# Rows of a mixture of experts moved as quarters of 96 words, turned by VectorE instead of TensorE

## The chip, the cores and the metric

The kernel runs on one core of one Trainium2 chip. The metric is device time of one execution in microseconds (us); the time shown is a median of three runs. The engines are TensorE (PE, with its weight loads PEld), VectorE (DVE), ScalarE (ACT), GpSimd (POOL) and SyncE (SP), which here only issues DMAs.

## The reference

Two stages in float32. The first is a gated recurrence for 4 batches, 8 heads, 768 steps, head size 48. Its output, as 3072 token rows of 384 words, goes through a two-level gate to one of 4 x 4 experts with 1024 hidden units.

```python
# stage 1, for each batch and head
state = alpha[t][:, None] * state + outer(k[t], v[t])
y[t] = q[t] @ state
# x = y as (3072, 384); stage 2
g_idx = argmax(x @ w_group);  g_w = softmax weight of g_idx
for g in range(4):
    e_idx = argmax(xg @ w_expert[g]);  e_w = its softmax weight
    for e in range(4):
        h = maximum(xg[mask_e] @ w1[g, e], 0.0)
        out[tok_idx] = (g_w * e_w)[:, None] * (h @ w2[g, e])
```

## The kernel before

The recurrence runs in 24 chunks of 128 steps, four batches one after the other. For each chunk the kernel forms 128 token rows of `xr` (`[128, 24, XW]`, 384 words, then the token's weight, then its number). The gate's choice gives every token a place in a table `slots_d` in device memory, one stretch of 3072 rows for each expert, and `scatter` writes the 128 rows of a chunk with one indirect DMA issued by POOL. Unused places were filled beforehand from `blank` with a token number out of range, so that such rows are not written in the end.

The experts follow as 17 jobs. Jobs 0 and 1 are both expert 0: its first 128 rows, which are read back early into `early_rows`, and up to 96 more. Jobs 2 to 16 are the other 15 experts in falling order of their counts, with room for 216 tokens in job 2, three fewer from job to job and 168 in the last. A loop after them takes what is left over; on this input it has no turn. For job j the program does this:

- `fetch_rows` (L768, SP) reads the job's rows, tokens on partitions, three jobs ahead; `load_weights` (L169, L171, SP) reads the weights, two jobs ahead, as soon as the buffer of job j - 2 is free.
- `columns` calls `turned` (L617): six TensorE transposes bring up to 2 x 112 rows into a layout with features on partitions; DVE copies them from PSUM to `xt_e` (L619). In the program this stands after `hidden` of the job before.
- `dst` (L804, DVE) is the row numbers for the output as integers, in one of two buffers.
- `hidden` (L632): 96 matmul rows of the profile's kind in four groups, each read by ACT's ReLU (L634) into `hT`. `result` (L647): 96 more, copied by ACT into `yT` (L649).
- `deliver_last` stands behind the first group of the next job's `hidden`: six transposes of `yT` back into rows (L659), two DVE multiplications by the weight (L664), two indirect DMAs from POOL into the output (L666).

Each engine works in program order (the order is written out by hand, no scheduler moves anything). SP's DMAs all go through one queue, POOL's indirect DMAs through another, and both are carried by the same 16 DMA engines.

Of the kernel before, what the change touches and what calls it, by code (L numbers as in the profile page):

```python
# [34 lines left out]
def gla_then_hierarchical_moe(  # L35
# [60 lines left out]
    XW = DM + 2  # L96
# [37 lines left out]
    part_f = iota("part_f", [P, 1], [[0, 1]], cm=1)  # L134
    token_f = iota("token_f", [P, NT], [[P, NT]], cm=1)
# [11 lines left out]
    nc.gpsimd.memset(blank.rearrange("p (t w) -> p t w", t=2)[:, :, DM + 1:XW], float(N))  # L147
# [6 lines left out]
    nc.gpsimd.tensor_copy(out=xr[:, :, DM + 1], in_=token_f)  # L154

    early_rows = cp.tile([P, FIXED, XW], F32, name="early_rows")
# [38 lines left out]
    with ExitStack() as gla:  # L195
# [175 lines left out]
        def to_rows(n, yt):  # L371
# [17 lines left out]
            if n + 1 == LAST:  # L389
                logits()  # L390
            nc.scalar.copy(out=x[:, bc, 0:DM].rearrange("s (p w) -> s p w", p=HP),
                           in_=z[:, :, 0:D2])
# [3 lines left out]
        def choose(b, c0, c1):  # L396
# [46 lines left out]
            nc.vector.reciprocal(out=x[:, c0:c1, DM], in_=cw)  # L443

        def send(b, c0, c1):
# [32 lines left out]
            def scatter(c):  # L478
# [134 lines left out]
    def turned(xg, xt, n, c0, copy=nc.vector.tensor_copy):  # L613

        z = bank()
        for dc in range(DC):
            nc.tensor.transpose(z[:, dc * P:dc * P + n], xg[0:n, dc * P:(dc + 1) * P],  # L617
                                ident[0:n, 0:n])
        copy(  # L619
            out=xt[:, :, c0:c0 + n],  # L620
            in_=z[:, 0:DM].rearrange("p (c t) -> p c t", c=DC)[:, :, 0:n])
# [16 lines left out]
    def result(w2, hT, n):  # L638

        yT = mp.tile([P, DC, CAP], F32, name="yT")  # L640
# [12 lines left out]
    out_by = deque(dram_disjoint_views(out, 2 * NE + 1))  # L653

    def deliver(yT, c0, n, weight, dst, by_act=False):
# [4 lines left out]
        yo = mp.tile([P, DM], F32, name="yo", bufs=3)  # L660
        if by_act:
            nc.scalar.activation(out=yo[0:n], in_=zy[0:n, 0:DM], func=AF.Copy, scale=weight)
        else:
            nc.vector.tensor_scalar(out=yo[0:n], in0=zy[0:n, 0:DM], scalar1=weight,  # L664
                                    scalar2=None, op0=ALU.mult)
# [4 lines left out]
    def columns(job, *copies):  # L670
        xt = mp.tile([P, DC, CAP], F32, name="xt_e")
        for t, (c0, n) in enumerate(job["parts"]):
            turned(job["rows"][:, t, :], xt, n, c0, *copies[t:t + 1])
        return xt

    def left_over():
# [20 lines left out]
        for of, total in ((excess, held), (ceiling, base)):  # L697
# [8 lines left out]
        nc.vector.tensor_scalar(out=first, in0=first, scalar1=float(P), scalar2=part_f,  # L706
                                op0=ALU.mult, op1=ALU.add)
        gone = rp.tile([P, NX], F32, name="gone")
        nc.vector.tensor_tensor(out=gone, in0=first, in1=held, op=ALU.is_ge)
        nc.vector.tensor_tensor(out=first, in0=base, in1=first, op=ALU.add)  # L710
        nc.vector.scalar_tensor_tensor(out=first, in0=gone, scalar=float(NE * N), in1=first,
                                       op0=ALU.mult, op1=ALU.add)
        n_more = rp.tile([P, 1], I32, name="n_more")
        nc.vector.tensor_copy(out=n_more, in_=ends[:, NE - 1:NE])
        return first, whose, n_more
# [35 lines left out]
    jobs = [dict(e=e, parts=[(0, EARLY)], rows=early_rows[:, e:e + 1, :]) for e in range(FIXED)]  # L751
    jobs += [dict(e=e, parts=[(0, CAP - EARLY)]) for e in range(FIXED)]
    jobs += [dict(r=r, parts=[(0, BLK), (BLK, cap(r) - BLK)]) for r in range(NS)]
# [9 lines left out]

    def fetch_rows(job):
        e, k = expert(job), len(job["parts"])
        c0, n = (EARLY, CAP - EARLY) if k == 1 else (0, BLK)
        job["rows"] = mp.tile([P, 2, XW], F32, name="xg", bufs=5)
        return nc.sync.dma_start(  # L768
            out=job["rows"][0:n, 0:k, :],
# [140 lines left out]
```

## Time and profile before

| | |
|---|---|
| three runs | 447.63, 448.93, 449.02 us; median 448.93 |
| profiled execution, its own time | 447.46 us |
| span of the profile, first to last instruction | 445.6 us |
| PE busy | 412.8 us (93% of the span) |
| DVE, ACT, POOL busy | 150.8, 124.9, 149.3 us |
| mean granted TensorE clock | 0.968 of full speed |
| moved by DMA | 95.35 MB, 214 GB/s on average |

The times below and in the rows are from the start of the span. The recurrence takes about the first 150 us, the expert jobs the rest, job 2 starting at 178.44 and job 16 at 418.52. The profiled execution is 1.47 us below the median of the runs, so sums are made against 447.46.

### The profile page before, as it was taken

To read this page: it belongs to the slowest core of one execution; us is meant where nothing else is said; L and a number is where in the kernel's file an instruction comes from. 1 tells how busy PE (TensorE), PEld (TensorE's weight loads), DVE (VectorE), ACT (ScalarE), POOL (GpSimd) and SP (SyncE) were. 2 spreads that over 40 slices of the span, in tenths; PEclk is the share of its full clock that TensorE was granted. 3 is DMA by queue.
4 is the path that set the end of the run, shared out by engine and by line. 5 is a ranking of instruction groups with operands and counts; after the bars stand their busy time and mean duration, and the time that the engine had idled before them with its cause. 6 is when DMAs were issued, how large, how long until landed. Compare 5 with 4: busy or idle time off the path is not lost.

```text
span 445.6 us, 8826 instructions
## 1 busy us (share of the span) xinstructions
PE 412.8 (93%) x3538; PEld 392.5 (88%) x3538; DVE 150.8 (34%) x437; ACT 124.9 (28%) x306; POOL 149.3 (34%) x197
## 2 busy tenths in 40 slices
PE   5998998988989797999999999999999999999990
PEld 4887887877878697999999999999999999999990
DVE  7768667678864620101172101011011011111100
ACT  1464645455556211211112111112112111112110
POOL 6886649579767500001201011022021012021111
PEclk9998988899989899999999999999999999999996
DMA  8999975696112369557546565586576486574000
GB/s 264 403 370 360 350 317 195 212 359 251 38 37 91 107 233 352 199 193 272 192 159 230 220 237 201 172 282 219 170 273 237 168 299 219 193 264 171 6 20 24
DMA packets 22506, 95.35 MB, mean 214 GB/s; under 512 B 5119, under 2 KB 9740, under 8 KB 17984
## 3 DMA queue, kind: packets, MB, share of 16 engines
q1 hardware_dynamic: 16448, 85.27, 53.2%
q0 software_dynamic: 6016, 9.50, 6.3%
q8 instruction: 29, 0.48, 0.5%
q14 instruction: 13, 0.11, 0.1%
HBM read 79.73 MB, written 15.10 MB: 213 GB/s over the span
## 4 chain that ended last, share of the span: by engine, by line
issue 57%; PE 21%; POOL 10%; DVE 7%; ACT 1%; DMA 1%; POOLq 0%; ACTq 0%; DVEq 0%
POOL out_dram L666 7%; PE bank L380 4%; PE bank L349 4%; PE bank L284 4%; PE bank L361 3%; PE bank L321 2%; DVE cq L270 2%; PE bank L309 1%; DVE rev L262 1%; PE bank L632 1%; POOL sm L297 1%; POOL qp L272 1%; POOL kp L265 1%; PE bank L164 1%; DVE gained L329 1%
## 5 line engine op out<-in xcount | busy, mean ns | idle before, releaser
L632 PE MATMUL bank<-xt_e,w 128*128 128x128 f32 (+16 forms) x816 | 136.4, 325 | 1.9 <-ACT xt_e L619 1.9
L632 PEld LDWEIGHTS bank<-xt_e,w 128*128 128x128 f32 x816 | 130.8, 193 | 2.3 <-ACT xt_e L619 2.3
L647 PE MATMUL bank<-hT,w 128*128 128x128 f32 (+16 forms) x816 | 132.5, 322 | 0.0
L647 PEld LDWEIGHTS bank<-hT,w 128*128 128x128 f32 x816 | 128.8, 190 | 0.1
L666 POOL DMA_INDIRECT out_dram<-yo,dst x32 | 36.7, 1148 | 243.3 <-DVE yo L664 228.2
L634 ACT ACTIVATE hT<-bank 128x256 f32<-128x256 f32 (+16 forms) x68 | 32.6, 479 | 112.1 <-PE bank L632 109.2
L664 DVE TENSOR_SCALAR yo<-bank,xg 112x384 f32<-112x384 f32 (+15 forms) x30 | 17.2, 611 | 116.0 <-PE bank L659 116.0
L649 ACT COPY yT<-bank 128x192 f32<-128x192 f32 (+32 forms) x34 | 13.3, 390 | 124.5 <-PE bank L647 124.5
L619 DVE COPY xt_e<-bank 128x336 f32<-128x336 f32 (+15 forms) x30 | 12.4, 456 | 83.0 <-PE bank L617 83.0
L284 PE MATMUL bank<-qp,kp 48*128 48x128 f32 x384 | 32.0, 302 | 5.6 <-POOL qp L272 5.6
L297 POOL TENSOR_SCALAR_AFFINE_SELECT sm<-sm 128x512 f32<-128x512 f32 x43 | 26.3, 632 | 28.1 <-ACT sm L296 28.1
L284 PEld LDWEIGHTS bank<-qp,kp 48*128 48x128 f32 x384 | 25.6, 199 | 10.2 <-POOL qp L272 5.8
L361 PE MATMUL bank<-sm,v 128*48 128x128 f32 (+1 forms) x384 | 31.9, 301 | 0.4
L380 PE MATMUL bank<-wr,yt 112*128 112x116 f32 x192 | 28.1, 291 | 1.3 <-ACT yt L368 1.1
L296 ACT COPY sm<-bank 128x512 f32<-128x512 f32 x43 | 23.3, 588 | 15.4 <-PE bank L284 13.8
L361 PEld LDWEIGHTS bank<-sm,v 128*48 128x48 f32 (+1 forms) x384 | 25.2, 144 | 2.6 <-POOL sm L297 1.2
L480 POOL DMA_INDIRECT slots_d<-xr,place x24 | 24.2, 1008 | 9.1 <-issue 4.5
L380 PEld LDWEIGHTS bank<-wr,yt 112*128 112x128 f32 x192 | 23.9, 196 | 3.7 <-ACT yt L368 2.5
L349 PE MATMUL bank<-qp,state 48*48 48x128 f32 (+1 forms) x320 | 24.6, 299 | 0.0
L270 DVE TENSOR_TENSOR_SCAN cq<-qka,starts 112x387 f32<-112x387 f32 x24 | 23.0, 959 | 2.5
L337 ACT ACTIVATE state<-gained,rev 112x48 f32<-112x48 f32 x64 | 16.2, 323 | 25.9 <-DVE gained L329 21.7
L272 POOL TENSOR_TENSOR qp<-qka,cq 112x384 f32<-112x384 f32 x24 | 21.9, 912 | 2.7 <-DVE cq L270 2.4
(116 smaller groups left out, 320.7 us busy)
## 6 DMA issues: line engine op xcount, KB each, us to landing
w<-in_w_dram SPq DMA_DIRECT2D x32, 1536.0 KB, 7.3
qka<-in_qka_dram SPq DMA_DIRECT2D x24, 578.0 KB, 9.7
slots_d<-blank SPq DMA_DIRECT2D x1, 5404.0 KB, 20.3
xg<-slots_d SPq DMA_DIRECT2D x15, 337.8 KB, 7.8
v<-in_v_dram SPq DMA_DIRECT2D x3, 1152.0 KB, 12.5
w<-in_qka_dram SPq DMA_DIRECT2D x4, 578.0 KB, 9.2
w<-in_qka_dram SPq DMA_DIRECT2D x4, 385.5 KB, 5.7
w<-in_qka_dram SPq DMA_DIRECT2D x4, 193.0 KB, 3.3
```

What stands on the lines that cost most here:

```text
L270: nc.vector.tensor_tensor_scan(out=flat(cq), data0=a[:, 0:W], data1=st, initial=1.0, op0=ALU.mult, op1=ALU.min)
L272: nc.gpsimd.tensor_tensor(out=qp, in0=q, in1=cq[:, :, 1:A1], op=ALU.mult)
L284: nc.tensor.matmul(z[i][:, p * P:(p + 1) * P], lhsT=kp[r, p, c, :], rhs=qp[r, p, c, :], start=True, stop=True)
L297: nc.gpsimd.affine_select(out=sm[:, i], in_=sm[:, i], pattern=[[0, HP], [1, P]], compare_op=ALU.is_ge, fill=0.0, base=0, channel_multiplie ...
L349: nc.tensor.matmul(z[o, p * P:(p + 1) * P], lhsT=st[r, p, 0:o.stop - o.start], rhs=qp[r, p, c, :], start=(p == 0), stop=False, skip_group_ ...
L361: nc.tensor.matmul(z[o, p * P:(p + 1) * P], lhsT=vs[b][:, bc, h * D:h * D + o.stop - o.start], rhs=sm[:, i, p, :], start=(p == 0 and bc == ...
L380: nc.tensor.matmul(z[:, p * W:(p + 1) * W], lhsT=yt[:, p, :], rhs=wr[:, p, :], start=True, stop=True)
L480: nc.gpsimd.indirect_dma_start(out=slots_by[t], out_offset=bass.IndirectOffsetOnAxis(ap=place[:, c:c + 1], axis=0), in_=x[:, c0 + c, :], i ...
L632: nc.tensor.matmul(z[:, k * n:(k + 1) * n], lhsT=w1[:, dc, f * P:(f + 1) * P], rhs=xt[:, dc, 0:n], start=(dc == 0), stop=(dc == DC - 1))
L634: nc.scalar.activation(out=hT[:, f0:f0 + 2, 0:n], in_=z[:, 0:2 * n].rearrange("p (f t) -> p f t", f=2), func=AF.Relu)
L647: nc.tensor.matmul(z[:, i * n:(i + 1) * n], lhsT=w2[:, f, dc * P:(dc + 1) * P], rhs=hT[:, f, 0:n], start=(f == 0), stop=(f == FC - 1))
L666: nc.gpsimd.indirect_dma_start(out=out_by.popleft(), out_offset=bass.IndirectOffsetOnAxis(ap=dst, axis=0), in_=yo[0:n], in_offset=None, bo ...
```

## The change

A token's row in `slots_d` becomes four quarters of 96 words, each followed by its own copy of the weight and its own number (`4 * token + quarter`): 392 words instead of 386. A job's rows are read with one DMA for each quarter, so that partition `32 j + t` holds quarter j of token t of each block of 32 tokens (`[128, blocks, 98]`; seven blocks for jobs 2 to 9, six for jobs 10 to 16). One VectorE instruction then transposes all the squares of 32 x 32 of a job; the feature order that results is other than before, and the host permutes the rows of `w1` and the columns of `w2` to suit. On the way back one VectorE transpose turns `yT` into quarters, one multiplication applies the weights, and each block of 32 tokens is written with an indirect DMA of 128 quarters of 96 words. Only the last job goes back as before, through TensorE, with a small extra load (`marks`) of weights and numbers. `yT` is two fixed buffers, zeroed once by POOL.

```diff
-    XW = DM + 2
+    QW = DM // 4 + 2
+    XW = 4 * QW
+    NB = CAP // 32
...
-    part_f = iota("part_f", [P, 1], [[0, 1]], cm=1)
-    token_f = iota("token_f", [P, NT], [[P, NT]], cm=1)
+    for j in range(4):
+        z = slice(32 * j, 32 * j + 32)
+        nc.gpsimd.iota(out=in_tile[z], pattern=[[32, 4]], base=0, channel_multiplier=1,
+                       allow_small_or_imprecise_dtypes=True)
+        nc.gpsimd.memset(quarter[z], float(j))
+    quarter_f = iota("quarter_f", [P, NT, 4], [[4 * P, NT], [1, 4]], cm=4)
...
-                    for e in range(FIXED):
-                        nc.sync.dma_start(out=early_rows[:, e, :],
-                                          in_=slots_d[e * N:e * N + EARLY, :])
+                    for j in range(4):
+                        nc.sync.dma_start(
+                            out=early_rows[32 * j:32 * j + 32],
+                            in_=slots_d[0:EARLY, j * QW:(j + 1) * QW].rearrange(
+                                "(b t) w -> t b w", t=32))
...
+    results = [rp.tile([P, DC, CAP], F32, name=f"yT{i}") for i in range(2)]
+    for t in results:
+        nc.gpsimd.memset(t, 0.0)
...
+    def deliver_quarters(job, yT, dst):
+
+        nb, rows = job["nb"], job["rows"]
+        yq = mp.tile([P, NB, DM // 4], F32, name="yq")
+        nc.vector.transpose(
+            out=yq[:, 0:nb].rearrange("p b (c r) -> p b c r", c=DC),
+            in_=yT[:, :, 0:32 * nb].rearrange("p c (b t) -> p b c t", t=32))
+        nc.vector.tensor_tensor(
+            out=yq[:, 0:nb], in0=yq[:, 0:nb],
+            in1=rows[:, 0:nb, QW - 2:QW - 1].to_broadcast([P, nb, DM // 4]), op=ALU.mult)
+        for b in range(nb):
+            nc.gpsimd.indirect_dma_start(
+                out=out_by.popleft().rearrange("n (j w) -> (n j) w", j=4),
+                out_offset=bass.IndirectOffsetOnAxis(ap=dst[:, b:b + 1], axis=0),
+                in_=yq[:, b, :], in_offset=None, bounds_check=4 * N - 1, oob_is_err=False)
 
-    def columns(job, *copies):
+    def columns(job):
         xt = mp.tile([P, DC, CAP], F32, name="xt_e")
-        for t, (c0, n) in enumerate(job["parts"]):
-            turned(job["rows"][:, t, :], xt, n, c0, *copies[t:t + 1])
+        nb = job["nb"]
+        nc.vector.transpose(
+            out=xt[:, :, 0:32 * nb].rearrange("p c (b t) -> p b c t", t=32),
+            in_=job["rows"][:, 0:nb, 0:DM // 4].rearrange("p b (c r) -> p b c r", c=DC))
         return xt
+
+    def destined(job):
+
+        nb, left = job["nb"], job["n"] % 32
+        dst = mp.tile([P, NB], I32, name="dst_q")
+        nc.vector.tensor_copy(out=dst[:, 0:nb], in_=job["rows"][:, 0:nb, QW - 1])
+        if left:
+            none = mp.tile([P, 1], F32, name="none")
+            nc.vector.tensor_scalar(out=none, in0=in_tile[:, 0:1], scalar1=float(left),
+                                    scalar2=float(4 * N), op0=ALU.is_ge, op1=ALU.mult)
+            nc.vector.tensor_tensor(out=dst[:, nb - 1:nb], in0=none,
+                                    in1=job["rows"][:, nb - 1, QW - 1:QW], op=ALU.add)
+        return dst
...
     def fetch_rows(job):
...
+        job["rows"] = mp.tile([P, NB, QW], F32, name="xq", bufs=5)
+        of = slots_d.rearrange("(e n) w -> e n w", e=NE)[ds(e, 1)]
+        for j in range(4):
+            dma = nc.sync.dma_start(
+                out=job["rows"][32 * j:32 * j + 32, 0:nb, :],
+                in_=of[:, c0:c0 + 32 * nb, j * QW:(j + 1) * QW].rearrange(
+                    "o (b t) w -> (o t) b w", t=32))
```

On TensorE an expert job before reads as follows (job 3, from its first matmul to the start of `result`; L632 is `hidden`, L659 the way back of job 2, L617 the way in of job 4).

```order
L632 MATMUL bank<-xt_e,w_2338 128x213 [waits DMAHW5_49,DVE_49]
L632 MATMUL bank<-xt_e,w_2338 128x213 x5
L659 MATMUL bank<-ident,yT 112x128 [waits Activation_49]
...
L659 MATMUL bank<-ident,yT 104x128 x2
L632 MATMUL bank<-xt_e,w_2338 128x213 [waits PE_49]
...
L617 MATMUL bank<-ident,xg 128x112 [waits DMAHW4_49,PE_49]
L617 MATMUL bank<-ident,xg 128x112 x2
L617 MATMUL bank<-ident,xg 128x98 [waits Activation_49]
L617 MATMUL bank<-ident,xg 128x98 x2
L647 MATMUL bank<-hT,w_2339 128x213 [waits DMAHW6_49,DVE_49]
```

And with the change, the same job (L639 is `hidden`, L655 `result`).

```order
L639 MATMUL bank<-xt_e,w_2362 128x213 [waits DMAHW4_49,DVE_49,PE_49]
L639 MATMUL bank<-xt_e,w_2362 128x213 x5
L639 MATMUL bank<-xt_e,w_2362 128x213 [waits PE_49]
...
L655 MATMUL bank<-hT,w_2363 128x213 [waits DMAHW5_49,Activation_49]
L655 MATMUL bank<-hT,w_2363 128x213
L655 MATMUL bank<-hT,w_2363 128x213 [waits Activation_49]
```

All twelve transposes are gone, and TensorE no longer waits itself for the rows' DMA.

On VectorE the same stretch reads with the change as follows: the transposes of the rows (L701), the output numbers (L710 to L715), the way back of the job before (L686, L689).

```order
L701 STREAM_TRANSPOSE xt_e<-xq 128x7x3x32 [waits DMAHW2_49,DMAHW1_49,DMAHW3_49,DMAHW0_49,PE_49]
L710 CAST dst_q<-xq 128x7 [waits DMASW4_49,DMASW3_49,DMASW5_49,DMASW2_49,DMASW7_49,DMASW1_49,DMASW0_49]
L713 TENSOR_SCALAR none<-in_tile 128x1
L715 TENSOR_TENSOR dst_q<-none,xq 128x1 [waits DVE_49]
L686 STREAM_TRANSPOSE yq<-yT_2160 128x672 [waits Activation_49]
L689 TENSOR_TENSOR yq<-yq,xq 128x672 [waits DVE_49]
L701 STREAM_TRANSPOSE xt_e<-xq 128x7x3x32 [waits DMAHW6_49,DMAHW1_49,DMAHW7_49,DMAHW0_49,PE_49]
```

The copy into `dst_q` waits for POOL's seven scatters (DMASW) that last used its buffer, those of two jobs before; behind it on VectorE stand the way back of the job before and the columns of the next.

On POOL the end of the first stage before reads as follows: the last two scatters of rows into `slots_d`, then the first one into the output.

```order
L480 DMA slots_d<-xr,place 49152x386 [waits DMASW6_49,Activation_49]
L480 DMA slots_d<-xr,place 49152x386 [waits DMASW7_49,DVE_49,Activation_49]
L666 DMA out_dram<-yo,dst 3072x384 [waits DMASW0_49,DVE_49,Pool_49]
```

With the change the two fixed `yT` buffers are cleared between them.

```order
L490 DMA slots_d<-xr,place 49152x392 [waits DMASW6_49,Activation_49]
L628 MEMSET yT_2159 128x672 [waits PE_49]
L628 MEMSET yT_2160 128x672
L490 DMA slots_d<-xr,place 49152x392 [waits DMASW7_49,DVE_49,Activation_49]
L693 DMA out_dram<-yq,dst_q 12288x96 [waits DMASW0_49,DVE_49,Pool_49]
```

The last chunk's scatter, for which the fetch of job 1's rows waits, now stands behind two memsets.

## Rows read from the trace of the kernel before

**Rows 1.** Window of job 6: length, busy us of each engine, PEclk, DMA share, GB/s.
```profile
251.60:269.40 17.80, 17.80 (x110) 17.73 (x109) 2.06 (x5) 2.88 (x6) 2.07 (x2) 1.00 0.59 215
```

**Rows 2.** Timeline of PE, job 5: start us, us, engine, line, count.
```profile
233.66 2.26 PE L632 MATMUL bank<-xt_e,w 128*128 128x207 f32 x12
...
235.76 0.82 PE L659 MATMUL bank<-ident,yT 128*112 128x128 f32 x6
...
236.42 6.47 PE L632 MATMUL bank<-xt_e,w 128*128 128x207 f32 x36
...
242.72 0.69 PE L617 MATMUL bank<-ident,xg 112*128 112x112 f32 x6
...
243.25 8.60 PE L647 MATMUL bank<-hT,w 128*128 128x207 f32 x48
...
251.68 2.23 PE L632 MATMUL bank<-xt_e,w 128*128 128x204 f32 x12
```

**Rows 3.** Timeline of PE, around the transposes in job 2 and job 15.
```profile
178.44 2.38 PE L632 MATMUL bank<-xt_e,w 128*128 128x216 f32 x12
...
187.55 0.71 PE L617 MATMUL bank<-ident,xg 112*128 112x112 f32 x6
...
188.10 8.95 PE L647 MATMUL bank<-hT,w 128*128 128x216 f32 x48
...
410.75 0.78 PE L617 MATMUL bank<-ident,xg 112*128 112x112 f32 x6
...
411.45 7.23 PE L647 MATMUL bank<-hT,w 128*128 128x171 f32 x48
418.52 1.87 PE L632 MATMUL bank<-xt_e,w 128*128 128x168 f32 x12
```

**Rows 4.** Timeline, the last two scatters of the first stage to job 1's end.
```profile
154.46 0.97 POOL L480 DMA_INDIRECT slots_d<-xr,place  x1 [0.30 <-issue]
...
155.74 1.06 POOL L480 DMA_INDIRECT slots_d<-xr,place  x1 [0.30 <-ACT hT L634]
...
159.27 0.34 SPq L768 DMA_DIRECT2D xg<-slots_d  x1
...
160.60 0.36 SPq L169 DMA_DIRECT2D w<-in_w_dram  x1
...
164.04 1.58 PE L632 MATMUL bank<-xt_e,w 128*128 128x96 f32 x12 [0.49 <-ACT xt_e L619]
...
172.50 0.75 PE L617 MATMUL bank<-ident,xg 112*128 112x112 f32 x6 [2.56 <-DMA xg<-slots_d]
```

**Rows 5.** Timeline, the start of the kernel.
```profile
2.79 0.13 POOL L130 IOTA floor_f<- 128x1 f32 x1
2.87 0.17 DVE L191 COPY starts<-desc_f 128x4 f32<-128x4 f32 x1 [1.23 <-POOL desc_f L130]
2.87 0.73 POOL L146 MEMSET blank<- 128x772 f32 x1
```

**Rows 6.** DMA issues to landing (count, median us): 149 to 157, 250 to 268, 286 to 300; q0 is POOL's queue.
```profile
slots_d<-xr,place POOLq DMA_INDIRECT x6, 3.0
...
q0 software_dynamic: 192, 0.31, 4.8%
...
out_dram<-yo,dst POOLq DMA_INDIRECT x2, 5.6
...
out_dram<-yo,dst POOLq DMA_INDIRECT x2, 9.9
```

**Rows 7.** Timeline of DVE: three kinds of instruction, and a wait of `dst`.
```profile
125.64 0.96 DVE L270 TENSOR_TENSOR_SCAN cq<-qka,starts 112x387 f32<-112x387 f32 x1
...
132.47 0.68 DVE L293 TENSOR_TENSOR sm<-bank,causal 128x512 f32<-128x512 f32 x1
...
225.07 0.87 DVE L619 COPY xt_e<-bank 128x336 f32<-128x336 f32 x2 [5.87 <-PE bank L617]
...
305.74 0.17 DVE L804 CAST dst<-xg 112x2 int32<-112x2 f32 x1 [8.74 <-issue]
```

More of the change, by code (lines that the diff above doesn't have):

```diff
@@ L390, in to_rows @@
                 logits()
-            nc.scalar.copy(out=x[:, bc, 0:DM].rearrange("s (p w) -> s p w", p=HP),
-                           in_=z[:, :, 0:D2])
+            nc.scalar.copy(out=quarters[:, n, :, 0:D2], in_=z[:, :, 0:D2])
             if n + 1 < LAST:
@@ L638, in result @@
     def result(w2, hT, n):
-        yT = mp.tile([P, DC, CAP], F32, name="yT")
+        yT = results[0]
+        results.reverse()
         for d0 in range(0, DC, 2):
@@ L651, in result, with row_of @@
         return yT
-    out_by = deque(dram_disjoint_views(out, 2 * NE + 1))
+    out_by = deque(dram_disjoint_views(out, NB * NE + 8))
+    def row_of(quarter, to):
+        nc.vector.tensor_scalar(out=to, in0=quarter, scalar1=0.25, scalar2=None, op0=ALU.mult)
     def deliver(yT, c0, n, weight, dst, by_act=False):
@@ L749, in by_number @@
         return order, excess, ceiling
-    jobs = [dict(e=e, parts=[(0, EARLY)], rows=early_rows[:, e:e + 1, :]) for e in range(FIXED)]
-    jobs += [dict(e=e, parts=[(0, CAP - EARLY)]) for e in range(FIXED)]
-    jobs += [dict(r=r, parts=[(0, BLK), (BLK, cap(r) - BLK)]) for r in range(NS)]
+    jobs = [dict(e=0, n=EARLY, rows=early_rows), dict(e=0, c0=EARLY, n=CAP - EARLY)]
+    jobs += [dict(r=r, c0=0, n=cap(r)) for r in range(NS)]
+    for job in jobs:
+        job["nb"] = -(-job["n"] // 32)
     def expert(job):
@@ L764, in fetch_rows @@
     def fetch_rows(job):
[L765 to L769, printed above, removed]
-            in_=slots_d.rearrange("(e n) w -> e n w", e=NE)[ds(e, 1), c0:c0 + k * n, :].rearrange(
-                "o (t p) w -> (o p) t w", t=k))
+        e, nb, c0 = expert(job), job["nb"], job["c0"]
+        job["rows"] = mp.tile([P, NB, QW], F32, name="xq", bufs=5)
[5 more added lines that the diff above has]
+                    "o (b t) w -> (o t) b w", t=32))
+        if job is jobs[-1]:
+            job["marks"] = mp.tile([P, 2, 2], F32, name="marks", bufs=1)
+            nc.sync.dma_start(
+                out=job["marks"][0:BLK],
+                in_=of[:, 0:2 * BLK, QW - 2:QW].rearrange("o (t p) w -> (o p) t w", t=2))
+        return dma
     last = None
     def deliver_last():
-        if last is not None:
-            job, yT, dst = last
-            for t, (c0, n) in enumerate(job["parts"]):
-                deliver(yT, c0, n, job["rows"][0:n, t, DM:DM + 1], dst[0:n, t:t + 1],
-                        by_act=t == 1 and job is jobs[-1])
+        if last is None:
+            return
+        job, yT, dst = last
+        if "marks" in job:
+            dst = mp.tile([P, 2], I32, name="dst_m")
+            row_of(job["marks"][0:BLK, :, 1], dst[0:BLK])
+            for t, n in enumerate((BLK, job["n"] - BLK)):
+                deliver(yT, t * BLK, n, job["marks"][0:n, t, 0:1], dst[0:n, t:t + 1],
+                        by_act=t == 1)
+        else:
+            deliver_quarters(job, yT, dst)
     def last_gates():
@@ L789, in gla_then_hierarchical_moe @@
     AHEAD = 3
-    xt = columns(jobs[0], nc.scalar.copy)
+    xt = columns(jobs[0])
     while late:
@@ L799, in gla_then_hierarchical_moe @@
                 fetch_rows(jobs[k])
-        e, (_, n), k = job["e"], job["parts"][0], len(job["parts"])
-        width = sum(w for _, w in job["parts"])
+        width = job["n"]
         w1, w2 = weights[0] if j < 2 * FIXED else weights.pop(j)
-        dst = mp.tile([P, 2], I32, name="dst")
-        nc.vector.tensor_copy(out=dst[0:n, 0:k], in_=job["rows"][0:n, :k, DM + 1])
+        dst = destined(job)
         hT = hidden(w1, xt, width, {2: [last_gates if j == 0 else deliver_last]})
@@ L815, in gla_then_hierarchical_moe @@
         if j + 1 < len(jobs):
-            xt = columns(jobs[j + 1], *([nc.scalar.copy] if j == 0 else []))
+            xt = columns(jobs[j + 1])
         if j == 4:
```

84 lines of the change are left out of this document (46 added, 38 removed).

## The prediction

> **What bounds the kernel now.** I read the page's busy shares first (PE 93%, DVE, ACT and POOL a third each), then the chain of waits, which is mostly "issue" on PE's side in the second half and so says little there, and then the windows by job. Job 6 shows why: PE is busy for all of its 17.80 us at the full granted clock, VectorE for 2.06 of them, POOL for 2.07, and the DMA engines for 0.59 of the time [rows 1]. So from job 2 to job 16, 240.08 us between their first matmuls (178.44 to 418.52 [rows 3]), time is the sum of what TensorE issues, and what leaves TensorE there leaves the time, as long as its results come from elsewhere early enough. The timeline of job 5 gives the sum: 12 matmuls from 233.66, six transposes from 235.76, 36 matmuls from 236.42, six transposes from 242.72, 48 matmuls from 243.25, the next job at 251.68 [rows 2]. I count from start to start, since the ends are modelled and overlap.
>
> **The change, part by part.** *Way back (L659).* The six transposes hold TensorE from 235.76 to 236.42, 0.66 us [rows 2]. Jobs 3 to 16 each carry six (0.65 to 0.66, 9.2 us in all), job 2 carries three, 0.3. The last job's own way back stays.
>
> *Way in (L617).* From 242.72 to 243.25, 0.53 [rows 2]. In jobs 2 to 15 this gap is 0.55 at first (187.55 to 188.10), falls to 0.47, and is 0.70 in the last two (the last from 410.75 to 411.45) [rows 3]; the fourteen make 7.6. What the transposes covered here is the last ReLU: `result` needs it only at its thirteenth matmul row of 48, 1.8 us after its start even in job 15 (12/48 of 411.45 to 418.52 [rows 3]); a ReLU or copy of ACT takes 2.88/6 = 0.5 [rows 1]. So no new wait takes the place.
>
> *VectorE instead.* A 32 x 32 transpose is in no row. Per element and partition the two-operand multiplication takes 0.68/512 = 1.33 ns, the copy from PSUM 0.87/672 = 1.29, the scan 0.96/387 = 2.48 [rows 7]. A job has 672 elements: bounded by 0 and the scan's 1.67 us, taken as 0.9, as the copies whose shape it shares. Way in, way back and multiplication are 2.7, the numbers 3 x 0.17 [rows 7] more; VectorE had 2.06 busy of 17.8 [rows 1], and keeps over 12 idle. It is hidden: the columns are needed only when `result` of the job before ends, 8 us after the transpose may start.
>
> *POOL.* Seven scatters of 128 quarters where there were two. In a row of scatters of 128 one starts 1.28 after the other (154.46 and 155.74: 0.97, a pause of 0.30 [rows 4]), so the seventh starts 7.7 after the first. Hidden too, with a condition that is the first rival.
>
> *DMA.* The bytes stay. For each job POOL's queue took 4.8% of 18 us, 0.86 us of all 16 engines [rows 6], and the fetch carries as much again, so about 1.8 of the 10.5 us (0.59 of 17.8) that the engines are busy [rows 1]. Pieces are a quarter as long: at no extra cost per piece it stays 1.8, at the full price of a long row for each it is four times that, 7.1. Busy time then lies between 10.5 and 15.9 us in a job that will last some 16.6; weights are asked for a whole job early. I take 12, nearer the lower end since the bytes are the same, and no cost. [...] No run here shows pieces so small with data in them.
>
> *Entry into the jobs.* The last scatter started at 155.74 [rows 4]. Ahead of it POOL now clears two buffers of 672 words: by `blank`'s 0.73 for 772 [rows 5], 0.64 each, 1.3 together. The fetch of job 1's rows moves from 159.27 to 160.6; three more issues of 0.34 follow, so the weights of job 2 leave at 162.9, not 160.60 [rows 4]. Job 2's rows, queued behind them, landed at about 172.5, when TensorE had waited 2.56 for them. They now land at 174.8, plus 0.4 for smaller pieces (bounds 0 and 2.7, three times the 0.9 that a job's fetch takes; the bytes stay, so near 0), plus 0.9 on VectorE: job 2 can start at 176.1. TensorE does not wait for them in the middle any more: job 1 starts at about 164.2 (164.04 [rows 4]; its rows land later, the fetch's last part at 163.8, plus a VectorE transpose of 0.4), and its 96 matmul rows take some 11 us (a little under 1.58 for twelve [rows 4]), so it is through at 175.2. So 176.1 against 178.44: a gain of 2.3, between 0 and 3.2, which TensorE's own 175.2 allows. SP then issues twelve fetches and only after them the weights of job 3; these are needed at about 193, 16 us of cover.
>
> The very first columns move from TensorE to VectorE, where they wait for the early rows ahead of the gate's last instructions. I put it at nothing: the last scatters are held by POOL's own row of six.
>
> *Start.* POOL makes its constants before VectorE may copy `desc_f` (VectorE waited 1.23 us for it, until 2.87). Seven more small instructions stand ahead, at the pace of 0.08 to 0.13 of an `IOTA` [rows 5]: 0.7 us, on the path to the first scan. Bounds 0 and 0.9, taken as 0.7.
>
> The sum: 9.2 + 0.3 + 7.6 + 2.3 - 0.7 = 18.7 us. The profiled execution took 447.46, so 428.8; it lies 1.47 below the median of the runs, and 448.93 - 18.7 = 430.2. I forecast 429.5.
>
> **Rival 1: the scatters become a chain (the side of slower).** `dst_q` has two buffers. The copy for job j waits until all scatters of job j - 2 have landed; VectorE does the way back of job j - 1 only behind it, and so POOL's next seven scatters stand behind the landing of the last seven. One turn of that chain is 7.7 for the issues, the landing, 0.5 for the numbers and 1.8 for transpose and multiplication. For the landing there are three rows: 3.0 us with the queues empty, 5.6 among weights, 9.9 in the worst job [rows 6]; that `dst` already waits for such a landing is seen at 305.74, where VectorE idled 8.74 [rows 7]. With 5.6 a turn is 15.6 with seven blocks and 14.3 with six, against jobs of 16.0 on average (240.08 less 16.4, over fourteen [rows 3]): about even, and the chain starts some 13 us ahead of need (a job of 16.4 less the 3.2 of VectorE work between the copy and the next job's columns). Jobs 3 to 15 last 206 us (223.7 less job 2's 17.6, from 178.44 to the end of its `result` near 197 less 0.9 [rows 3]), and thirteen turns must stay below 206 + 13. Five of them have six blocks: with x for a turn of seven, 13 x - 6.4 < 219, x < 17.3, a landing of 7.3 (5.8 if each of the two VectorE instructions took its upper bound, 1.5 more together). Beyond it each microsecond of landing costs 13; the whole gain is gone at a landing of 8.7. With 9.9 it is 13 x 19.9 - 6.4 - 219 = 33 us: 462. For it: landings of up to 9.9 exist, and there are seven scatters for two. Against it: the 9.9 belong to a job whose second part has 89 rows, and every scatter is now of 128, as those of the first stage with 3.0. I give a landing between 7.3 and 8.7 (430 to 447) 0.12, beyond that 0.09.
>
> [...]
>
> **Rival 2: the entry eats its gain.** The memsets wait for a TensorE release, the early columns hold up the gate on VectorE, or small pieces land 2.8 later. Then job 2 starts at 178.8, as before, and the time is 429.5 + 2.7 = 432. It is 0.15 of the main case's chance and inside its own range, 426 to 433.
>
> **Rival 3: no change.** TensorE would have to idle where it transposed, because weights or columns come late by 1.2 us in each job. The weights of job j + 2 leave when job j's buffer is free and have a whole job; at the upper bound of 15.9 us busy in 16.6 they would be just in time, in the last jobs not quite. Chance 0.04, 448.
>
> **How the numbers follow.** Main case 0.69, 426 to 433; less than 426, if the start costs nothing and the entry gives all, 0.06; rival 1 0.12 and 0.09; rival 3 0.04. A range of 425.5 to 440 leaves out the 0.09, the 0.04, a third of the 0.12 and 0.03 below: 0.20. About 0.3% (1.3 us) is what this kernel's runs can tell from no change. Faster: 0.69 + 0.06 + 0.12 less 0.01 at its edge, 0.86; same 0.05; slower 0.09.
>
> **What would show it.** Right: in the jobs PE still busy for the whole window, `hidden` following `result` without a gap, job 5 shorter by 1.19; job 2 starting near 176; VectorE's transposes near 0.9; `dst_q` copied within a job's first half; POOL's scatters 1.28 apart. Wrong: idle PE ahead of `hidden` released by VectorE, with `dst_q` waiting before it (rival 1); scatters further apart than 1.28; PE waiting for weights (rival 3); a transpose several times 0.9, which would lengthen the same chain as rival 1.

## The result and the profile after

The changed kernel takes 429.94 us (median of four runs, 428.59 to 431.24); the kernel before, beside it, 448.98 (447.63 to 449.58). The ratio is 0.958, with an interval of 0.9535 to 0.9624: faster, and 0.4 us from the forecast. The experiments ran in three batches, each on one chip and beside the kernel before (medians 448.59, 446.71 and 452.27 us), so their times can be compared within a batch to some two microseconds (the intervals of most ratios are 0.4% wide to either side) and across batches less well; in the third the changed kernel ran once more, with a ratio of 0.9524 (0.9483 to 0.9566). The profiled execution of after is one of the two longer ones, 431.07 us with a span of 429.3, so the two profiles lie only 16.4 us apart. I judge the steps on that difference.

I begin where the sum begins, with TensorE in a job. The timeline of PE in job 5 and 6 of after answers to [rows 2] (start, us, engine, line, count):

```profile
234.30 8.56 PE L639 MATMUL bank<-xt_e,w 128*128 128x207 f32 x48
242.70 8.56 PE L655 MATMUL bank<-hT,w 128*128 128x207 f32 x48
251.10 8.44 PE L639 MATMUL bank<-xt_e,w 128*128 128x204 f32 x48
259.38 8.44 PE L655 MATMUL bank<-hT,w 128*128 128x204 f32 x48
```

No row stands between `hidden` and `result`, and none has a wait. (Each of the two is 48 matmul rows of the profile, 96 together; "The kernel before" gives 96 to each.) Job 5 takes 16.80 us (234.30 to 251.10) where it took 18.02. The window of job 6 answers to [rows 1] (length; busy us of PE, PEld, DVE, ACT, POOL; granted clock; DMA share; GB/s):

```profile
251.10:267.66 16.56, 16.56 (x98) 16.56 (x97) 2.91 (x6) 2.88 (x6) 6.82 (x7) 1.00 0.74 231
```

TensorE is still busy for the whole window, POOL went from 2.07 to 6.82 us. The DMA share is 0.74 of 16.56, that is 12.3 us; the forecast took 12.

VectorE of after, at the start of job 4, answers to [rows 7]:

```profile
215.97 0.17 DVE L710 CAST dst_q<-xq 128x7 int32<-128x7 f32 x1 [12.80 <-DMA out_dram<-yq,dst_q]
...
217.89 0.88 DVE L686 STREAM_TRANSPOSE yq<-yT 128x672 f32<-128x672 f32 x1 [1.50 <-ACT yT L657]
218.80 0.86 DVE L689 TENSOR_TENSOR yq<-yq,xq 128x672 f32<-128x672 f32 x1
219.57 0.87 DVE L701 STREAM_TRANSPOSE xt_e<-xq 128x672 f32<-128x672 f32 x1
```

The transposes take 0.87 and 0.88 us. The numbers' copy waits 12.80 us for the scatters of two jobs before, and yet the transpose behind it waits 1.50 more for ACT: the chain of rival 1 is there, and TensorE is not held by it.

The landings, that is the times from a scatter's issue to the last update of its semaphore, answer to [rows 6] (first the page, then the tile view of the output, then two single scatters and the tile view of before):

```profile
q1 hardware_dynamic: 27360, 85.10, 58.1%
q0 software_dynamic: 4816, 9.55, 6.8%
...
out_dram<-yq,dst_q POOLq DMA_INDIRECT x99, 5.8
```

```profile
L693 POOL DMA_INDIRECT out_dram<-yq,dst_q x99: 967/974/1038, 167.7 to 414.3; - x99
...
DMA to landing us min/median/max: 2.2/5.8/7.8
```

```profile
220.20 2.20 POOL L666 DMA_INDIRECT out_dram<-yo,dst  x1 [0.31 <-issue]
...
342.70 0.91 POOL L666 DMA_INDIRECT out_dram<-yo,dst  x1 [0.30 <-issue]
...
DMA to landing us min/median/max: 2.8/5.6/14.5
```

The median landing is 5.8 us against 5.6, the longest 7.8 against 14.5. The view of after could assign a landing to 12 of its 101 scatters only; the semaphore records of the 90 that start before 400 us give 2.2 to 7.9 us, with a median of 5.5. Each scatter costs POOL 0.97 us, where before single ones cost up to 2.20 (the one at 220.20 has 101 rows, the one at 342.70 has 80).

Two stretches did not go as forecast. The first is the entry, which answers to [rows 4] (a bracket is the idle time ahead and what ended it; SPq is SP's queue of issues):

```profile
147.16 1.75 SPq L497 DMA_DIRECT2D early_rows<-slots_d  x4
...
151.42 0.99 POOL L490 DMA_INDIRECT slots_d<-xr,place  x1 [4.72 <-DVE starts L418]
...
157.58 1.29 POOL L628 MEMSET yT<- 128x672 f32 x2
...
159.04 0.97 POOL L490 DMA_INDIRECT slots_d<-xr,place  x1 [0.17 <-issue]
162.07 1.73 SPq L820 DMA_DIRECT2D xq<-slots_d  x4
164.79 0.38 SPq L178 DMA_DIRECT2D w<-in_w_dram  x1
...
165.89 13.90 SPq L820 DMA_DIRECT2D xq<-slots_d  x12
165.95 5.57 PE L639 MATMUL bank<-xt_e,w 128*128 128x96 f32 x48 [1.91 <-DVE dst_q L710]
...
178.42 0.88 DVE L701 STREAM_TRANSPOSE xt_e<-xq 128x672 f32<-128x672 f32 x1 [11.49 <-DMA xq<-slots_d]
```

The second is job 2 itself (PE timeline; then windows of that stretch with the granted clock third from the right), which answers to [rows 3]:

```profile
179.40 11.99 PE L639 MATMUL bank<-xt_e,w 128*128 128x216 f32 x48 [2.52 <-issue]
191.22 8.92 PE L655 MATMUL bank<-hT,w 128*128 128x216 f32 x48
```

```profile
179.40:182.00 2.60, 2.60 (x7) 2.44 (x8) 1.81 (x5) 0.00 (x0) 0.97 (x1) 0.50 0.82 158
182.00:185.00 3.00, 3.00 (x10) 2.75 (x10) 0.00 (x0) 0.53 (x1) 1.95 (x2) 0.50 0.92 336
185.00:191.20 6.20, 6.20 (x34) 6.17 (x33) 0.39 (x3) 1.06 (x2) 0.00 (x0) 0.96 1.03 371
```

Job 2 starts at 179.40, behind two waits of TensorE (1.91 and 2.52 us), and its first 5.6 us run at a granted clock of 0.50, the lower of the two levels, 1.00 and 0.50, that the clock records of before and after hold. Its `hidden` takes 11.82 us from start to start, some 3.0 more than the 8.9 of its `result` would suggest.

Set beside each other, from start to start (the profile of after less that of before; the first line is contained in the second, and so not in the sum):

| stretch | forecast | measured |
|---|---|---|
| first matmul of all (6.41, was 5.38) | +0.7 | +1.03 |
| start of job 2 (179.40, was 178.44) | -1.6 | +0.96 |
| job 2 | -0.85 | +2.1: about -0.9, and +3.0 by the clock |
| jobs 3 to 15 (205.44, was 221.63) | -15.6 | -16.19 |
| job 16 up to its own way back | -0.66 | -0.65 |
| behind that | 0 | -2.5 |
| sum | -18.7 | -16.2 of the span |

### The profile page after: what moved, and what is told of

The parts are those of the page before. It is cut to its first block, busy times and chain, and to the rows that moved or that the text cites. A ratio compares the mean times of both kernels' runs of the same rounds, so it can differ in the third digit from the quotient of the medians.

```text
span 429.3 us, 8796 instructions
## 1 busy us (share of the span) xinstructions
PE 396.3 (92%) x3352; PEld 376.9 (88%) x3352; DVE 163.8 (38%) x457; ACT 124.4 (29%) x304; POOL 213.4 (50%) x275
## 4 chain that ended last, share of the span: by engine, by line
PE 55%; issue 3%; POOL 2%; DMA 1%; DVE 0%; SPq 0%; POOLq 0%; ACT 0%; DVEq 0%; ACTq 0%
PE bank L639 28%; PE bank L655 27%; POOL out_dram L693 1%; DMA slots_d<-xr,place 1%; DMA xq<-slots_d 0%; POOL out_dram L678 0%; POOL yT L628 0%; SPq L820 0%; DVE yq L686 0%; DVE yq L689 0%; POOLq L885 0%; ACT yT L657 0%; DVE dst_q L710 0%; DVE xt_e L701 0%; POOLq L678 0%
## 5 line engine op out<-in xcount | busy, mean ns | idle before, releaser
L693 POOL DMA_INDIRECT out_dram<-yq,dst_q x99 | 96.4, 974 | 158.8 <-DVE yq L689 120.1
L639 PE MATMUL bank<-xt_e,w 128*128 128x128 f32 (+16 forms) x816 | 136.8, 329 | 6.0 <-issue 4.1
L639 PEld LDWEIGHTS bank<-xt_e,w 128*128 128x128 f32 x816 | 133.7, 196 | 6.9 <-issue 6.5
L655 PE MATMUL bank<-hT,w 128*128 128x128 f32 (+16 forms) x816 | 131.8, 321 | 0.0
L655 PEld LDWEIGHTS bank<-hT,w 128*128 128x128 f32 x816 | 129.6, 190 | 0.0
L710 DVE CAST dst_q<-xq 128x7 int32<-128x7 f32 (+2 forms) x16 | 2.7, 166 | 160.0 <-DMA out_dram<-yq,dst_q 160.0
L305 ACT COPY sm<-bank 128x512 f32<-128x512 f32 x43 | 23.3, 588 | 15.6 <-PE bank L293 14.0
L346 ACT ACTIVATE state<-gained,rev 112x48 f32<-112x48 f32 x64 | 16.2, 323 | 26.1 <-DVE gained L338 21.9
L274 POOL TENSOR_TENSOR kp<-qka,rev 112x384 f32<-112x384 f32 x24 | 22.4, 934 | 1.1 <-DVE rev L271 0.9
```

The lines of the kernel that those rows point to most:

```text
L305: nc.scalar.copy(out=sm[:, i], in_=z[i])
L639: nc.tensor.matmul(z[:, k * n:(k + 1) * n], lhsT=w1[:, dc, f * P:(f + 1) * P], rhs=xt[:, dc, 0:n], start=(dc == 0), stop=(dc == DC - 1))
L655: nc.tensor.matmul(z[:, i * n:(i + 1) * n], lhsT=w2[:, f, dc * P:(dc + 1) * P], rhs=hT[:, f, 0:n], start=(f == 0), stop=(f == FC - 1))
L693: nc.gpsimd.indirect_dma_start(out=out_by.popleft().rearrange("n (j w) -> (n j) w", j=4), out_offset=bass.IndirectOffsetOnAxis(ap=dst[:, b ...
```

## The experiments

All are edits of the changed kernel but the last. "Start of job 16" and the like are starts of its first matmul.

**Is it TensorE's issue time?** `turns_in` and `turns_both` put back transposes that nobody needs; VectorE goes on doing the work.

```diff
+            if j > 1:
+                idle_turns(6, 104)
             xt = columns(jobs[j + 1])
```
```diff
+        hT = hidden(w1, xt, width, {2: [last_gates if j == 0 else deliver_last] + (
+            [partial(idle_turns, 6, P)] if j > 2 else [])})
```

> The changed kernel, with six extra TensorE transposes (unneeded; nobody reads them) behind the hidden layer of jobs 2 to 15, where the old way in stood; VectorE still does the real work. If the gain of the way in is TensorE's issue time alone, as my sum had it (14 gaps of 0.53 to 0.55, 7.6 us), this costs 7 to 7.6 us against the changed kernel: about 437 us. If TensorE was not the bound there any more and VectorE's chain sets the pace, they fall into waits and cost nothing: 430 us.

> As the run before, and six more unneeded transposes behind the first group of the hidden layer of jobs 3 to 16, where the old way back stood. By TensorE's issue time: 7.6 plus 14 times 0.66 is 16.8 us, 446 to 447 us, so nearly all of the change's gain is undone with the rest of the change in place. If the gain comes from elsewhere (the entry, the end, the clock): less than half of that.

Measured: 437.78 us (436.09 to 438.27) and 447.03 (443.19 to 450.96), so 7.8 and 17.1 above the changed kernel. The PE timeline of `turns_both` in job 6:

```profile
253.81 2.23 PE L639 MATMUL bank<-xt_e,w 128*128 128x204 f32 x12
255.88 0.82 PE L667 MATMUL bank<-ident 128*128 128x128 f32 x6
256.54 6.38 PE L639 MATMUL bank<-xt_e,w 128*128 128x204 f32 x36
262.75 0.70 PE L667 MATMUL bank<-ident 104*128 104x104 f32 x6
263.29 8.47 PE L655 MATMUL bank<-hT,w 128*128 128x204 f32 x48
```

The gaps are 0.66 and 0.54, those of [rows 2]. Jobs 3 to 15 take 212.72 us with the first six and 221.26 with all twelve, against 205.44 without and 221.63 before. So of the 16.19 us that these jobs gained 15.82 are TensorE's issue time; where the other 0.37 come from is not shown. The rest of the change costs the jobs nothing.

**How near is the chain through `dst_q`?** Two and four extra scatters in jobs 2 to 15, into a table that nobody reads (`range(2)` and `range(4)`); then four again with more buffers (the last two lines; in the same run the quarters `yq` get three buffers).

```diff
+            for b in range(4):
+                nc.gpsimd.indirect_dma_start(
+                    out=spare_by.popleft().rearrange("n (j w) -> (n j) w", j=4),
...
-        dst = mp.tile([P, NB], I32, name="dst_q")
+        dst = mp.tile([P, NB], I32, name="dst_q", bufs=4)
```

> The changed kernel, with two extra scatters for each of jobs 2 to 15 of the same quarters into a table in device memory that nobody reads, behind the real ones. The copy into the output numbers must wait for these too. Rival 1's formula: a turn of the chain grows by 2 times 1.28, from about 15.6 to 18.2 us with seven blocks, which is beyond the 17.3 at which the lead of 13 us is used up: 13 times 18.2 less 6.4 less 219 is 11 us, about 441 us, with TensorE waiting for VectorE in the last third of the jobs. If the chain has more lead than I reckoned, or a new scatter does not wait for the landing of those two jobs before: 430 us.

> As the run before with four extra scatters in each job. Rival 1's formula: a turn of 20.7 us, 13 times 20.7 less 6.4 less 219 is 44 us: about 474 us, and the slope from two to four extra is 13 turns for each microsecond. POOL's own time, eleven scatters 1.28 apart, is 14.1 us in a job of 16: if only POOL's busy time counts, no cost, 430 us.

> As scatters_4 (four extra scatters for each of jobs 2 to 15 into a table that nobody reads), but with four buffers instead of two for the output numbers and three for the quarters. If the cost of scatters_4, some 46 us, is the chain through the two buffers of output numbers, it goes here but for POOL's own pace: eleven scatters 1.28 apart are 14.1 us in a job of 14 to 17, so 430 to 440 us. If the cost is the DMA engines' load or POOL's, it stays: over 460 us.

Measured: 433.26, 476.36 and 436.09 us. With four extra the chain has TensorE; VectorE and then PE of `scatters_4`:

```profile
257.02 0.17 DVE L719 CAST dst_q<-xq 128x7 int32<-128x7 f32 x1 [17.60 <-DMA spare_d<-yq,dst_q]
...
257.36 0.87 DVE L688 STREAM_TRANSPOSE yq<-yT 128x672 f32<-128x672 f32 x1
...
277.37 0.17 DVE L719 CAST dst_q<-xq 128x7 int32<-128x7 f32 x1 [17.46 <-DMA spare_d<-yq,dst_q]
...
297.52 0.17 DVE L719 CAST dst_q<-xq 128x7 int32<-128x7 f32 x1 [17.25 <-DMA spare_d<-yq,dst_q]
```

```profile
319.29 8.04 PE L639 MATMUL bank<-xt_e,w 128*128 128x192 f32 x48 [2.29 <-issue]
327.16 7.96 PE L655 MATMUL bank<-hT,w 128*128 128x192 f32 x48
339.64 10.68 PE L639 MATMUL bank<-xt_e,w 128*128 128x189 f32 x48 [4.52 <-issue]
```

A turn is 20.35 and 20.15 us (the formula said 20.7), the transpose behind the copy waits for nothing any more, and TensorE idles ahead of `hidden` from job 10 on, as the lead is used up. With four buffers all of that is gone: jobs 3 to 15 take 205.44 us again, and `dst_q` waits for nothing:

```profile
L688 DVE STREAM_TRANSPOSE yq<-yT 128x672 f32<-128x672 f32 (+3 forms) x16 | 12.7, 796 | 177.4 <-ACT yT L657 177.4
...
L719 DVE CAST dst_q<-xq 128x7 int32<-128x7 f32 (+2 forms) x16 | 2.1, 131 | 0.1
```

(group rows: busy us, mean ns, idle time ahead and its releaser). So some 40 of the 46 us are the chain through these buffers, not POOL's or the DMA engines' load. Of the 46, jobs 3 to 15 lost 26.6 (they take 232.07 us), part of it in a longer `hidden` behind the waits, by my estimate at a lower clock (10.68 us above, where the same shape takes 7.84 in after; the mean granted clock is 0.928 in this execution, 0.962 in after's), the tail of the last job, where POOL is still busy with the jobs before, 13.7, and the drain at the end 4.6 (below); with four buffers 1.4 of the tail and the drain's 4.6 stay. The run gave more buffers to the numbers and to the quarters together; that it is the numbers' pair which binds is read from the wait, which stands at their copy.

With two extra my formula missed: jobs 3 to 15 take 205.44 us there too. From 296.91 on, when the wait for ACT is as good as used up, two turns of seven blocks and two extra are 15.9 and 17.3 us, and five of six blocks and two extra 14.9 on average (330.12 to 404.51), where I had 18.2 and 16.9: the landing that closes a turn is that of the job's last scatter, and the extra ones land in 3.7 at the median, not in 5.6. The 3.3 us that `scatters_2` costs lie behind the jobs: 2.3 in the drain at the very end (below), 1.3 between the last scatter and that drain.

**The entry.** Three edits of it. `zero_later` clears the result buffers behind the last scatters:

```diff
-    for t in results:
-        nc.gpsimd.memset(t, 0.0)
...
         while outgoing:
             scatter()
+        for t in results:
+            nc.gpsimd.memset(t, 0.0)
```

`rows_first` fetches job 2's rows ahead of its weights:

```diff
-        for k in range(2 if j == 1 else j + AHEAD, j + AHEAD + 1):
+        for k in range(3 if j == 1 else j + AHEAD, j + AHEAD + 1):
...
+            fetched = fetch_rows(jobs[2]).ins.name
```

`fill_idle` gives TensorE unneeded work between job 1 and job 2:

```diff
+        if j == 1:
+            busy(24)
```

> The changed kernel with the two memsets of the result buffers on POOL behind the last scatters of the first stage instead of between them. By my step (two memsets of 0.64 us ahead of the last scatter) the rows of jobs 1 and 2 come 1.3 to 1.5 us earlier: job 2 starts at 177.9 to 178.1, the time falls by 1.4 us to about 428.5. If the four early fetches hold the scatters and the memsets only fill that wait, nothing changes.

> The changed kernel with the rows of job 2 fetched ahead of the weights of job 2, in the same queue. If TensorE's wait of 2.5 us ahead of job 2 is for these rows behind the weights, job 2 starts at about 177, 2.4 us earlier, provided that its weights are there too; and if the drop of the granted clock to 0.50 in job 2 (3.0 us) comes from the two waits just ahead of it, it may go as well: 424.5 to 427.5 us. If the weights then come late by as much, nothing is gained: 430 us.

> The changed kernel with 24 unneeded TensorE operations between job 1 and job 2, where TensorE waited 2.5 us for job 2's rows; nobody reads them. If the drop of the granted clock to 0.50 for 6.8 us in job 2 follows from TensorE's idle stretches ahead of it, job 2 runs at full clock and the time falls by about 3 us to 427, since the extra work lies in a wait. If the drop has another cause it stays, and the time is 430 us or a little more.

Measured, in one batch: 429.55, 426.40 and 433.25 us. In `zero_later` the last scatter starts at 158.20, job 1 at 164.97 and job 2 at 178.20, so the memsets do hold the entry by 1 us, as the expectation had it. Its ratio to before, 0.9629 (0.9594 to 0.9664), cannot be told from the changed kernel's 0.958, so the total shows nothing of it. In `rows_first` the wait ahead of job 2 is gone:

```profile
163.50 5.57 PE L639 MATMUL bank<-xt_e,w 128*128 128x96 f32 x48 [1.89 <-DVE dst_q L710]
168.90 5.52 PE L655 MATMUL bank<-hT,w 128*128 128x96 f32 x48
174.26 8.95 PE L639 MATMUL bank<-xt_e,w 128*128 128x216 f32 x48
183.05 8.92 PE L655 MATMUL bank<-hT,w 128*128 128x216 f32 x48
```

From job 1 to job 2 it takes 10.76 us instead of 13.45, and the weights of job 2, now issued second, are there in time. (The 2.4 us by which job 1 itself is earlier come from the first stage, which differs from execution to execution: job 0 starts at 148.90 here and at 151.33 in after, and this profile has fewer stretches at the lower clock ahead of it: 0.96 on average over the first 150 us, 0.94 in after.) It is the fastest of the three by 3 us, and inside what was expected of it. `fill_idle` shows job 2 at full clock (1.00 from 170 to 190) behind a TensorE without that wait:

```profile
171.57 5.52 PE L655 MATMUL bank<-hT,w 128*128 128x96 f32 x48
176.93 5.55 PE L173 MATMUL bank<-ident 128*128 128x128 f32 x48
182.32 8.93 PE L639 MATMUL bank<-xt_e,w 128*128 128x216 f32 x48
191.08 8.92 PE L655 MATMUL bank<-hT,w 128*128 128x216 f32 x48
```

The filling is 5.4 us long, twice the wait, and what the clock gives back (3.1) the filling takes (2.9): its span is 429.2, as after's 429.3. The expected 427 was missed, since I had not counted that length.

**The start, and all of it together.** `start_first` makes `desc_f` and `floor_f` ahead of POOL's new constants; `best` is `start_first`, `zero_later` and `rows_first` in one; `after_again` is the changed kernel unaltered, in their batch.

```diff
+    desc_f = iota("desc_f", [P, 4], [[-1, 4]], base=4)
+    floor_f = iota("floor_f", [P, FIXED], [[N, FIXED]], base=EARLY)
     in_tile = cp.tile([P, 4], F32, name="in_tile")
```

> The changed kernel once more, unaltered, on the chip of the three runs beside it, as the measure for them: 430 us, 427 to 431.5. If the 3 us of lowered clock in job 2 belong to this kernel's waits they stand in its trace again, behind the waits of 1.9 and 2.5 us; if they are a chance of one execution, job 2's hidden layer takes 8.9 us here.

> The changed kernel with the two constants that the first VectorE instructions wait for made ahead of POOL's new ones. If the first stage starts late by POOL's seven new instructions, the first matmul moves back from 6.41 to 5.4 us and the time falls by 1.0 us, to about 429. If something behind it takes up the microsecond (the loads of the first chunk): 430 us, with the first matmul earlier all the same.

> The changed kernel with three edits of the entry and the start together: those two constants first, the result buffers cleared behind the last scatters, job 2's rows fetched ahead of job 2's weights. By the single runs: 1.0 for the start, about 1 for job 1 starting earlier, 2.6 for the wait ahead of job 2 and 3 for the clock: 422 to 423.5 us. If the clock's 3 us come back (job 1 still has a wait ahead of it): 425 to 426.

Measured: 431.26 us (428.70 to 433.46), 432.41 (430.70 to 435.87), 429.81 (428.04 to 432.17). The PE timeline of `after_again`:

```profile
170.26 7.20 PE L639 MATMUL bank<-xt_e,w 128*128 128x96 f32 x48 [2.03 <-DVE dst_q L710]
177.29 5.52 PE L655 MATMUL bank<-hT,w 128*128 128x96 f32 x48
182.82 9.00 PE L639 MATMUL bank<-xt_e,w 128*128 128x216 f32 x48
```

Here the lowered clock fell into job 1 (7.20 us instead of 5.57; 0.72 on average from 170 to 176), which made TensorE late enough not to wait for job 2's rows at all; job 2 runs at full clock (1.00 from 182 to 194). So the place and the 3 us of the first profile belong to that execution. That there is such a stretch does not. Three more profiles, `zero_later` (where `hidden` is L637), `scatters_4_free` and `start_first`:

```profile
178.20 10.68 PE L637 MATMUL bank<-xt_e,w 128*128 128x216 f32 x48 [2.30 <-issue]
...
166.58 7.20 PE L639 MATMUL bank<-xt_e,w 128*128 128x96 f32 x48 [2.55 <-DVE dst_q L719]
...
183.03 9.00 PE L639 MATMUL bank<-xt_e,w 128*128 128x216 f32 x48 [1.12 <-issue]
```

Nine profiles have the changed kernel's order of fetches ahead of job 2. In five of them (after, `turns_in`, `turns_both`, `scatters_4`, `zero_later`) the lowered clock stands in job 2 (0.83 on average from 170 to 190 in after, 0.91 in the others), behind a wait of 2.3 to 2.5 us, and costs 1.5 to 1.7 us there, in after 3.0. In three (`after_again`, `scatters_2`, `scatters_4_free`) it stands in job 1, at 1.6 us, and job 2 then waits for nothing (in the last for 0.18). Only `start_first` has it in neither job. The three profiles without the wait ahead of job 2 (`rows_first`, `fill_idle`, `best`) have it in neither. In `start_first` the first matmul moves from 6.41 to 5.78, and job 2 starts no earlier (183.03 against 182.82): the start's microsecond is taken up inside the first stage. `best` starts job 2 at 181.30 and has the ratio 0.9496 (0.9456 to 0.9536) to before, against 0.9524 (0.9483 to 0.9566) of `after_again`: 1.5 us that these medians cannot tell from nothing, and far from the 7 to 8 that I had added up from single profiles. The traces say more of the entry itself: from the first matmul of job 1 to that of job 3 it takes 28.31 us in `rows_first` and 28.24 in `best`, and 29.94 to 34.03 in the nine profiles with the old order, so fetching the rows first is worth at least 1.6 us there.

**The end.** The last thing in the program is a drain on POOL (L973, in before L906). The views leave it out; the trace's own instruction records give it:

| kernel | indirect DMAs from POOL | drain, us |
|---|---|---|
| before | 56 | 4.65 |
| after (and all edits of it with 125) | 125 | 1.63 |
| `scatters_2` | 153 | 3.92 |
| `scatters_4`, `scatters_4_free` | 181 | 6.20 |
| `before_52` | 108 | 2.11 |

`before_52` is the kernel before, with 52 extra gathers of weights into an unread buffer:

```diff
+        for _ in range(spare.popleft() if len(out_by) < 2 * NE - 3 and spare else 0):
+            unread = mp.tile([P, 96], F32, name="unread", bufs=4)
+            nc.gpsimd.indirect_dma_start(
+                out=unread[0:n], out_offset=None,
+                in_=w1_d.rearrange("e p (x w) -> (e p x) w", w=96),
```

> The kernel before, with two extra indirect DMAs from POOL behind each of 26 of its scatters, 52 in all: each reads rows of 96 words of the weights into a buffer that nobody reads. POOL's last instruction before the end (a drain) took 4.65 us with 56 indirect DMAs in the program (before), 1.63 with 125 (the change), 3.92 with 153, 6.20 with 181 (two and four extra scatters): 0.0817 us for each DMA, starting anew somewhere between 56 and 125; the four fit 0.0817 times (count + 1), less 106 once past it. By that the drain is 0.25 us here (108 + 1 - 106 = 3) and the kernel with more work is 4.4 us faster at its end. If the drain goes by something else than the count of DMAs (rows, bytes, the scatters' form), it stays at 4.65 or grows, to 8.9 by the slope without a new start.

Measured: 464.02 us (457.80 to 466.42), its drain 2.11. Both expectations are half wrong. More DMAs made the drain shorter, so it does not simply grow with their number. If it starts anew somewhere, then not after 106 DMAs whatever they are, since that gave 0.25: at 0.0817 us for each, 2.11 is some 25 DMAs, so here the new start would lie near the 83rd. What sets it (rows, bytes, the kind) stays open. That the kernel lost 12 us in jobs 3 to 15 has another reason: its `dst` copies wait 112.1 us in all for the gathers, and behind them TensorE waits 8.8 us for VectorE, the same chain in the old kernel.

## Why the prediction was right

**The sum over the jobs held.** It named 17.1 us of TensorE issue in jobs 2 to 16, read start to start from [rows 2, 3]; jobs 3 to 15 gave 16.19 where 15.6 were forecast for them, job 16 0.65 where 0.66 were. The idle transposes of `turns_both` take 15.82 of the 16.19 back. No wait took the place of the way in: `result` follows `hidden` without a gap.

**VectorE and DMA held.** The transpose was priced at 0.9 from rows of the same shape; it is 0.88. Its time goes by the elements of a partition: 288 take 0.48 us (at 165.32), 576 take 0.77 (at 302.36) and 672 take 0.88, which is 1.04 ns for each further one, and the multiplication of 672 takes as long (0.86). The DMA engines were busy for 12.3 us of a job against 12.

**Rival 1 was there, and had more room than I reckoned.** Two extra scatters in each job cost the jobs nothing; four cost jobs 3 to 15 26.6 us. What was mis-sized is the landing that closes a turn: 5.6 in my sum, about 3.6 by the six-block turns of `scatters_2` (14.9 less seven issues of 1.28 and the 2.3 of VectorE). That `scatters_4` came near its 474 us is luck: the formula put 44 us into the jobs, and 18 of the 46 measured lie behind them. The long landings did not come: after's longest is 7.8. The 9.9 of [rows 6] is the middle of two landings, 5.8 us with 112 rows and 14.0 with 89. Of before's 32 scatters into the output the five that take POOL longest, 2.20, 2.05, 1.96, 1.81 and 1.65 us, have 101, 89, 83, 71 and 59 rows, all prime, and they are also the five that land last, after 14.5, 14.0, 13.9, 9.9 and 7.8 us; the other 27 take 0.91 to 1.43 and land after 2.8 to 7.0. In after all but the last job's two have 128. What makes those counts slow is not shown. For the scatters the shorter pieces show no cost: POOL's queue took 6.8% of 429.3 us against 6.3% of 445.6 for the same bytes, 1.1 us more in the whole kernel, and the median landing is 5.8 us for 5.6, though a scatter now carries fewer bytes (128 rows of 96 words, where most had 112 or fewer of 384).

**The entry failed.** Of its steps the memsets were sized right (1.29 for 1.3). What failed first is "I put it at nothing: the last scatters are held by POOL's own row of six". That row itself starts behind the early fetches, whose table it writes: in the trace's own records POOL's waits ahead of the first of the six name all four of them. They issue from 147.16 for 1.75 us, where one took 0.33; the last lands at 150.47, and the scatter starts at 151.42. Before, the one fetch landed at 148.53 and the scatter started at 149.34. (The bracket names a VectorE instruction, but the scatter follows the last of these waits by 0.74 us in both kernels.) Of the 2.1 us between the two starts 0.8 are the start's (job 0 began at 151.33, was 150.56), so the early fetches cost 1.3. No run of its own takes them away.

What failed second is the 0.4 us for job 2's rows in smaller pieces. My sum counted three more issues for job 1's rows and none for job 2's own, which leave in four issues as well, the first at 165.89 and the last at 167.69, 1.8 us apart. The last lands 10.6 us after its issue, and the single one before took as long (161.67 to 172.36): the pieces cost nothing in flight, the issues cost 1.8. So these rows landed at 178.29 instead of 175.2; the start accounts for 0.8 of that, the early fetches and the four issues for 1.3 each beyond what was forecast (the rest of the way was 0.3 shorter). Rival 2's outcome came true, with causes that it did not name in this form, and gave 2.5 us less than the main case.

**Two terms that I did not have made up for it.** The lowered clock in job 2 added 3.0 us in the profiled execution, and the shorter drain took away 3.0. The second stands in every profile with 125 indirect DMAs. Of the first only the size is chance: seven of the other eight profiles with this entry lose 1.5 to 1.7 us in job 1 or 2, one loses nothing. Two of after's four runs are 2.4 us shorter than the profiled one, which a clock stretch more or less would explain, but only one of the four has a profile, so that is not shown. Without the shorter drain the entry's miss would show in the median: 429.9 + 3.0 is 433, rival 2's 432. So the jobs were right by their mechanism, and that the total came within 0.4 us of the forecast is luck.

## What to carry to other kernels

Where one engine issues without a gap, price a removed instruction by the distance from start to start of its neighbours, and test the claim by putting idle ones back. The seams between stages need the opposite care: here job 2's rows in four issues of SP's queue, and four early readers of a table that a later writer waits for, cost 1.3 us each beyond what was forecast, and adding up what single profiles promise there gave 8 us of which 1.5 were left. When a buffer pair closes a loop through a DMA's landing, work out the turn, then add load until it binds, so that you know how much room is left (here two more scatters in each job cost the jobs nothing, and four cost them 26.6 us).

## What was unexpected in the hardware

- POOL's drain at the end took from 1.63 to 6.20 us. From 125 to 153 to 181 indirect DMAs it grew by 0.0817 us for each; yet with 56 it took 4.65, and with 108 of mixed kinds 2.11, so it does not simply grow with the count. What sets it is not shown.
- Stretches at a lower granted clock stand in the profiles of all these kernels (mean granted clock 0.928 to 0.977), and change place from one to the next. A wait of 2.56 us in before [rows 4] was followed by a full clock (1.00 from 176 to 182), one of 1.91 in after by a full one too (1.00 from 165 to 171), one of 2.52 there by 0.50, and in `after_again` the lower clock came within job 1 (0.72 on average from 170 to 176). In `rows_first` a wait of 1.89 ahead of job 1 was followed by a `hidden` of 5.57 us, as in after at full clock.
- SP took 13.90 us to issue twelve fetches behind one another (165.89), where four took 1.73. In the trace's own records eleven of the issues took 0.32 to 0.54 us. The sixth took 4.05, for a reason that is not shown, and ahead of the eighth SP waited 3.3 us, until a load of job 2's weights that uses the same semaphore had landed (177.12): here an issue far ahead of need waited itself.
